# Two 64-row turns of a recurrent attention and FFN kernel on VectorE in 32x32 blocks

## Chip, cores and metric

The kernel runs on one core of a Trainium2 chip. The metric is the device time of one execution in microseconds: 785.76 us before the change, the median of three runs (785.73 to 786.29). A change under 0.2%, some 1.6 us, is about the least that such a measurement can tell.

## What is computed

An attention of the RWKV7 kind with a state of 40x40 per batch and head, over 768 steps, and then an FFN on its output, all in float32 (4 batches, 8 heads, D = 40, 3072 tokens of 320 features, 2048 hidden):

```python
for t in range(S):                                  # S = 768
    y[:, :, t] = einsum('bhd,bhde->bhe', rt, state)
    Sa = einsum('bhde,bhe->bhd', state, at)
    state = state * wt[:, :, None, :] - einsum('bhd,bhe->bhde', Sa, bt)
    state = state + einsum('bhd,bhe->bhde', vt, kt)
x = y.transpose(0, 2, 1, 3).reshape(B * S, H * D)   # 3072 x 320
h = x @ w_in                                        # 320 x 2048
g = h * clip(h + 3.0, 0.0, 6.0) / 6.0
out = g @ w_out                                     # 2048 x 320
```

## The kernel before

The steps are cut into chunks of 64. A **unit** is one chunk of two batches, with their 8 heads; there are 24 units (0 to 23), four to a group of 128 steps (two chunks by two batch pairs), six groups. Tokens lie on the 128 partitions (64 of each batch), so what is loaded has to be turned until the 40 features of a head lie on the partitions: two heads side by side, in slots of 64 rows. In the main loop (units 4 to 23 as `own`) such turns are TensorE transposes. `turn_pairs` (L486) does 128x128 at a time, four to a unit, for W, K and the state; `turn_halves` (L496) does 64x64 at a time in 64-row tiles, eight to a unit, for R, V, A and B.

A unit's work is in stages. **Ahead** of its turn: W (turn of w, two scans by VectorE that give the cumulative gammas), gam (gammas `gam` and inverse gammas `rgam`, by POOL), A (L609: turned a times gam, `at`), B (turned b times rgam), K, F and E (masked scores), factor (L664: the inverse gammas turned back, times k and b by POOL), EV. The 32x32 blocks of a whole group are inverted by VectorE (`invert`, with 60 dependent operations at L769 and L775 between transposes at L749, L778 and L783), spread over the work of other units, and joined by TensorE in 32-row tiles. **Own** stages, which need the state of the unit two before: RT (L857: turn of r, copied by ACT at L862, and the fading of the state, by POOL and VectorE), VT (turn of v), R, C, S, U, UT, rS, H, ysn (L1021: 64 matmuls that give the new state and the output), then `move` and `move2` (L1068, L1073): 4 and 4 DMAs that lay the unit's output out as the FFN's input `xt`.

**The FFN** is a stream of 48 jobs, half the hidden width of one unit each. `expand` (L1118 to L1153) is 16 matmuls of 128x128x128 and, for the last 64 of the 320 features, 8 "short" ones (`short`, L1128) in 64x128 tiles, two tiles in turn; then relu and a minimum with product by ACT (L1139) and VectorE (L1140) into `gt`. `contract` (L1165) is matmuls of 320 columns from `gt`. `feed` puts pieces of this stream between the blocks of attention work, at rates written by hand.

**The order** is written by hand (a manual schedule). The loop has four blocks to a unit (BLOCKS), and in each, `a_block` collects the stages that fall due by OWN_STAGES (from the unit's first block), AHEAD_STAGES or CLOSE_STAGES and hands them to `together`. That issues TensorE's products in the order of PRODUCTS: first those of TURNS (W, S, K) in 128-row tiles, then at FIRST_NARROW the short matmuls of the expand before, then the products in 64-row tiles. What follows the products (evacuations by VectorE, ACT and POOL, and DMA issues) is issued in the order of RESULTS, as soon as five PSUM banks would be passed or the block's products are out. Each engine works through its own queue in order.

**DMAs** of the loop are nearly all issued by SyncE (SP), one queue in order: `fetch` (L452 to L471) loads R and V in four DMAs (L467) and W, A, B and K in two (L470); each single-buffered tile is fetched for the next unit right after its last use in the code, so R in RT, A in A, B, K and V in factor. The xt moves and the output stand in the same queue. Before the loop, a plan by hand (PLAN) works through group 0 and prepares group 1; the fetch of R for unit 4 stands in it at BEGIN + 2.

Of the kernel before, what the change touches and what calls it, by code (L numbers as in the profile page):

```python
# [31 lines left out]
def kernel(  # L32
# [183 lines left out]
    inputs, others = {}, {}  # L216
    for name in "WABK":
        inputs[name] = padded(const.tile([P, H, SLOT], F32, name=name), name)
    seconds()
    for name in "BK":  # L220
        others[name] = second(name)
# [9 lines left out]
    inputs["R"] = padded(const.tile([P, H, SLOT], F32, name="R"), "R")  # L231

    RR = const.tile([P, 2, NPR * D + SLOT - D], F32, name="RR")
    nc.gpsimd.memset(RR[:, :, NPR * D:], 0.0)
# [209 lines left out]
    def fetch(name, i, engine=None):  # L444

        if i is None or i >= NK:
            return
        x, crossed = {"W": (w, 0), "A": (a, 0), "B": (b, 0), "K": (k, 0), "R": (r, 1),
                      "V": (v, 1)}[name]
        if name == "V":  # L450
            t = values[i % AHEAD]
        else:  # L452
            t = placed.get((name, i))
            if (name, i) == ("R", 1):
                t = others["K"]
            if (name, i) == ("W", NU + 1):
                t = values[NU]
            t = t if t is not None else (others if i < 2 * NU and i % 2 and name != "R" else inputs)[name]
        g, p = names[i]
        engines = engine or nc.sync  # L460
        for q in range(2):
            engine = engines[q] if isinstance(engines, tuple) else engines
            y = x[2 * p + q, :, g * BL:(g + 1) * BL, :]
            rows = slice(q * BL, (q + 1) * BL)
            if crossed:
                for s in range(2):
                    engine.dma_start(out=t[rows, 4 * s:4 * s + 4, 0:D],  # L467
                                     in_=y[s::2].rearrange("h t e -> t h e"))
            else:
                engine.dma_start(out=t[rows, :, 0:D], in_=y.rearrange("h t e -> t h e"))  # L470
        data[i][name + "N"] = t  # L471
# [29 lines left out]
    def by_banks(x):  # L501
        return x[:].rearrange("p r (q t) -> p q r t", q=2)

    def turn_in(x, halves):

        return turn_halves(x)[2:] if halves else [turn_pairs(x)]
# [25 lines left out]
    def begun_beside():  # L532

        begin = -(-(SCAN + 1) // 16) * 16
        for n, name in enumerate("KB"):
            x = area[:, begin + n * H * JOIN:begin + (n + 1) * H * JOIN]
            nc.gpsimd.memset(x, 0.0)
            beside[name] = x.rearrange("p (h t) -> p h t", h=H)
        beside["E"] = grp.tile([P, H, BL], F32, name="E", tag="U", bufs=1)
        nc.gpsimd.memset(beside["E"][:], 0.0)  # L540

    def masked(o, x=None):
        if x is None:
# [6 lines left out]
    def prepare(i, F):  # L550
# [25 lines left out]
        def gam_stage():  # L576

            prods, wm = o["prods"], o["wm"]
            first = start[:].rearrange("p (n i) -> p n i", i=HB + 1)[:, :, 0]
            nc.vector.reciprocal(first, prods[:].rearrange("p r m i -> p (r m) i")[:, ::-1, HB])  # L580
            back = _ap(wm, SCAN, [[-1, SCAN]])
            nc.vector.tensor_tensor_scan(out=back, data0=back, data1=start[:], initial=0.0,  # L582
                                         op0=ALU.mult, op1=ALU.add)
            nc.vector.memset(first, 1.0)
            gam = o["G"] = grp.tile([P, NPR, P], F32, name="gam", tag="gam", bufs=NU + 2)
            rgam = o["rg"] = placed.get(("rgam", i)) or tmp.tile([P, NPR, P], F32, name="rgam", bufs=2)
# [12 lines left out]
            nc.gpsimd.tensor_copy(gv[:, :, HB:BL], o["prods"][:, :, 1, 0:HB])  # L599
            nc.gpsimd.tensor_copy(rv[:, :, 0:HB], o["prods"][:, :, 0, 0:HB][:, :, ::-1])  # L600
            dec = grp.tile([P, 2, 2, NPR], F32, name="dec", tag="dec", bufs=NU + 2)
            nc.gpsimd.tensor_copy(dec[:].rearrange("p m q r -> p r q m"),
                                  o["prods"][:].rearrange("p (r q) m i -> p r q m i", q=2)[:, :, :, :, HB])
            o["dec"] = dec
            if NU + 1 < i <= 2 * NU:
                fetch("V", i)
            yield from ()

        def a_stage():  # L609
            x = turn_in(o["AN"], halves)  # L610
            yield PE
            nc.vector.memset(_ap(o["wm"], 0, [[HB + 1, 2 * NB + 1]]), 0.0)  # L612
            at = o["at"] = grp.tile([P, NPR, P], F32, name="at", tag="at")
            for y, z, g in zip(parts_of(at, halves), x, parts_of(o["G"], halves)):
                nc.vector.tensor_tensor(out=y, in0=z, in1=g, op=ALU.mult)
            fetch("A", following(i))

        def b_stage():
# [45 lines left out]
        def factor_stage():  # L664
# [23 lines left out]
            for x, name in enumerate("KB"):  # L688
# [5 lines left out]
            if i > 2 * NU:  # L694
                fetch("V", i)
            for name in "BK":
                fetch(name, following(i))

        def k_stage():
            x = turn_pairs(o["KN"])  # L700
            yield PE
            kt = o["kt"] = turned("kt")
            nc.vector.tensor_tensor(out=kt[:], in0=x[:], in1=o["rg"][:], op=ALU.mult)

        def e_stage():
            x = scores(o["kt"], o["at"])
# [141 lines left out]
    def step(i):  # L848
# [6 lines left out]
        m = {}  # L855

        def s_RT():  # L857
            x = turn_in(o["RN"], halves)
            yield PE
            m["RT"] = turned("RT")  # L860
            for y, z in zip(parts_of(m["RT"], halves), x):
                nc.scalar.activation(out=y, in_=z, func=AF.Copy)  # L862
            if i and i != NU - 1:
                fetch("R", i + 1)
            if fresh:
                nc.gpsimd.tensor_copy(last_dec[p][:], dec[:, 1])
                return
# [2 lines left out]
            nc.gpsimd.tensor_copy(last_dec[p][:], dec[:, 1])  # L870
            nc.vector.tensor_tensor(out=st[:, :, :, 0:D], in0=st[:, :, :, 0:D],
                                    in1=_ap(scale[:], 0, [[NPR, 2], [1, NPR], [0, D]]), op=ALU.mult)

        def s_R():

# [195 lines left out]
        def s_move2():  # L1071
            for dst, src in m["moves"][4:]:
# [1 line left out]
            ready[i] = m["xt"]  # L1074
            yield from ()

        return {"RT": s_RT, "R": s_R, "VT": s_VT, "S": s_S, "U": s_U, "C": s_C, "UT": s_UT,
                "rS": s_rS,
                "sn": s_sn, "ysn": s_ysn, "H": s_H, "y": s_y, "move": s_move, "move2": s_move2}

# [37 lines left out]
    def expand(xt, j0, gts):  # L1118
# [6 lines left out]
                             stop=(begun[c] == 3 * NQ - 1))  # L1125
            begun[c] += 1

        def short():  # L1128
            narrow.clear()
            for i in range(NQ):  # L1130
                for c in range(2):
                    add(c, i, win2[half(c), (j0 + i) * P:(j0 + i + 1) * P], xt[half(c), 2, :])
            if begun[0] + begun[1] == 6 * NQ:
                results()

        def results():
            for c in range(2):
                gt = ffn.tile([P, NQ, P], F32, name="gt", bufs=5)
                nc.scalar.activation(out=gt[:], in_=hp[c][:], func=AF.Relu, bias=three[:], scale=1.0)  # L1139
                nc.vector.scalar_tensor_tensor(out=gt[:], in0=gt[:], scalar=6.0, in1=hp[c][:],  # L1140
                                               op0=ALU.min, op1=ALU.mult)
# [252 lines left out]
    for _ in range(18):  # L1394
# [21 lines left out]
    FIRST_NARROW = PRODUCTS[len(TURNS)]  # L1416

    def together(stages):

# [35 lines left out]
    def a_block(m):  # L1455

        if coming and begins[coming[0]] == m:
            u = coming.popleft()
            close = coming and begins[coming[0]] < m + BLOCKS
            ahead[u, m] = prepared(u), CLOSE_STAGES if close else AHEAD_STAGES  # L1460
        if m % BLOCKS == 0 and m // BLOCKS + NU < NK:
            i = m // BLOCKS + NU
            own[i, m] = step(i), OWN_STAGES
        parts = {}, {}
        for (u, begin), (fs, order) in sorted(own.items()) + sorted(ahead.items()):
            if m - begin < len(order):
                for name in order[m - begin]:
                    parts[begin % BLOCKS > 0].setdefault(name, []).append(fs[name])
# [15 lines left out]

    m = 0
    begun_beside()
    for i in range(NU, NK):
        spread[0] = i >= 2 * NU - 1
        for j in range(BLOCKS):
# [58 lines left out]
```

## Time and profile before

| | |
|---|---|
| Median of three runs | 785.76 us |
| The profiled execution | 785.4 us |
| Its span (first to last instruction) | 783.7 us |
| Mean granted TensorE clock | 0.965 |
| VectorE stream transposes L749, L778, L783 (128x1024), mean | 2.16, 1.97, 2.05 us |
| L496 turns of R, of A (TensorE matmuls of 64x64) | 160, 128 |
| ACT copies of the turned R, L862 | 22 of 0.597 us |
| SP's issue of one fetch DMA, median, L467 / L470 | 0.608 / 0.633 us |
| Fetches of R / of A in the whole kernel | 92 / 37 DMAs |

How to read the views: the page gives each engine's busy time and share of the span, and then, in 40 slices of about 19.6 us, the busy share of each in tenths. PE is TensorE's matmuls, PEld its weight loads, which run beside them; PEclk is the clock that TensorE was granted, in tenths. Lines such as L1021 are those of the kernel printed above. A list of waits gives what an engine stood idle for, with the instruction that released it: us in total, times, longest. A timeline has the start in us, the length, engine, line and operation with its tiles, and "x8" for eight records drawn as one; a group's records overlap, so its length and the start of the next group can differ. SPq is SP's queue of DMA issues.

### The profile page before, as it was taken

Reading aid. Unit: us, or ns where it says so; the run is one execution under the profiler, and the core shown is the slowest. Engines: PE = TensorE matmul, PEld = TensorE weight load, DVE = VectorE, ACT = ScalarE, POOL = GpSimd, SP = SyncE. Lnnn points to the kernel's source line nnn. Section 1 sums busy time; section 2 is a strip of 40 time slices with the busy share of each in tenths; the row PEclk is TensorE's granted clock in tenths of the full one; section 3 lists DMA queues with packets and bytes.
Section 4 is the critical chain, followed back from the end, with each engine's and each line's share of the span. In section 5 each row is a group of like instructions: output and inputs, shape, how many; then the busy total and the mean of one; then the engine's idle time right before and its main releaser. Section 6 shows DMA issues by size and latency. Waiting matters only on the chain.

```text
span 783.7 us, 32780 instructions
## 1 busy us (share of the span) xinstructions
PE 725.0 (93%) x14552; PEld 613.3 (78%) x14552; DVE 486.6 (62%) x951; ACT 320.2 (41%) x664; POOL 171.9 (22%) x321
## 2 busy tenths in 40 slices
PE   5636788999999989999999999999999999999998
PEld 3625677878878778888788888888888888888886
DVE  7899967688546699345888336887436972223110
ACT  2386865324445334443334543334543234412211
POOL 6403111222232304121304212203212111110000
PEclk9855899999999999999999999999999999999999
DMA  9684554311333312223213223213221101110000
GB/s 123 116 202 123 113 168 69 68 27 35 58 59 63 67 33 48 50 49 66 41 38 58 46 51 64 44 30 60 49 55 39 26 5 30 30 29 10 12 20 18
DMA packets 174205, 44.87 MB, mean 57 GB/s; under 512 B 157424, under 2 KB 172784, under 8 KB 174064
## 3 DMA queue, kind: packets, MB, share of 16 engines
q1 hardware_dynamic: 169760, 42.03, 27.5%
q8 instruction: 115, 1.88, 1.0%
q10 hardware_dynamic: 4304, 0.74, 0.6%
q14 instruction: 26, 0.21, 0.1%
HBM read 34.08 MB, written 3.93 MB: 49 GB/s over the span
## 4 chain that ended last, share of the span: by engine, by line
PE 77%; DVE 10%; issue 6%; DMA 2%; ACT 2%; POOL 2%; SPq 1%; POOLq 0%; ACTq 0%; DVEq 0%
PE h L1124 27%; PE o L1165 25%; PE pair L1021 4%; PE pair L524 4%; PE pair L496 2%; PE one L486 2%; DVE prods L571 2%; PE pair L884 2%; PE pair L925 1%; PE pair L717 1%; DVE prod L769 1%; PE pair L964 1%; DVE x L775 1%; PE pair L980 1%; PE one L906 1%
## 5 line engine op out<-in xcount | busy, mean ns | idle before, releaser
L1124 PE MATMUL h<-xt,win 128*128 128x128 f32 (+1 forms) x2304 | 248.7, 281 | 4.5 <-DVE gt L1140 4.5
L1124 PEld LDWEIGHTS h<-xt,win 128*128 128x128 f32 (+1 forms) x2304 | 229.3, 191 | 22.6 <-issue 4.2
L1165 PE MATMUL o<-wout,gt 128*128 128x320 f32 x768 | 230.5, 443 | 0.0
L1165 PEld LDWEIGHTS o<-wout,gt 128*128 128x128 f32 x768 | 138.4, 190 | 50.9 <-issue 0.2
L1140 DVE SCALAR_TENSOR_TENSOR gt<-gt,h 128x512 f32<-128x512 f32 x96 | 62.0, 680 | 73.4 <-ACT gt L1139 73.4
L1139 ACT ACTIVATE gt<-h,three 128x512 f32<-128x512 f32 x96 | 62.9, 687 | 102.8 <-PE h L1124 102.3
L546 DVE COPY_PREDICATED area<-mask,pair 128x512 f32<-128x512 int32 x56 | 40.4, 724 | 62.2 <-PE pair L524 52.8
L769 DVE TENSOR_TENSOR prod<-x 128x30 f32<-128x30 f32 (+9 forms) x180 | 65.5, 364 | 8.9 <-POOL x L754 3.3
L775 DVE TENSOR_TENSOR x<-x,prod 128x30 f32<-128x30 f32 (+9 forms) x180 | 64.3, 357 | 5.5
L1029 POOL TENSOR_TENSOR yg<-ys,gam 128x512 f32<-128x512 f32 x20 | 25.4, 1272 | 126.1 <-DVE ys L1028 83.2
L690 POOL TENSOR_TENSOR KBt<-K,rgt 128x320 f32<-128x320 f32 x22 | 19.1, 870 | 151.4 <-ACT rgt L679 139.9
L571 DVE TENSOR_TENSOR_SCAN prods<-area,start 128x528 f32<-128x528 f32 x24 | 40.8, 1703 | 9.7 <-ACT area L567 9.6
L1028 DVE TENSOR_TENSOR ys<-pair,ys 128x512 f32<-128x512 f32 x20 | 13.8, 690 | 49.8 <-PE pair L1021 40.8
L862 ACT ACTIVATE RT<-pair 128x512 f32<-128x512 f32 x22 | 13.1, 597 | 54.5 <-PE pair L496 54.4
L722 ACT ACTIVATE EV<-pair 64x320 f32<-64x320 f32 x44 | 18.9, 430 | 36.9 <-PE pair L717 36.5
L1021 PE MATMUL pair<-area,KBt 64*64 64x104 f32 x1280 | 33.1, 252 | 0.0
L1183 ACT ACTIVATE ob<-o 128x320 f32<-128x320 f32 x22 | 9.6, 437 | 56.2 <-PE o L1165 37.8
L837 ACT ACTIVATE tinv<-pair 32x256 f32<-32x256 f32 x48 | 18.0, 375 | 34.7 <-PE pair L827 34.2
L582 DVE TENSOR_TENSOR_SCAN area<-area,start 128x528 f32<-128x528 f32 x24 | 31.1, 1297 | 0.8
L1021 PEld LDWEIGHTS pair<-area,KBt 64*64 64x64 f32 x1280 | 29.1, 133 | 1.4
L950 POOL COPY area<-V 128x320 f32<-128x320 f32 x20 | 9.1, 455 | 84.6 <-DVE area L612 52.9
L600 POOL COPY rgam<-prods 128x256 f32<-128x256 f32 x22 | 24.9, 1131 | 0.0
(286 smaller groups left out, 1049.9 us busy)
## 6 DMA issues: line engine op xcount, KB each, us to landing
V<-in_v_dram SPq DMA_DIRECT2D x96, 40.0 KB
out_dram<-ob SPq DMA_DIRECT2D x47, 80.0 KB
R<-in_r_dram SPq DMA_DIRECT2D x92, 40.0 KB
B<-in_b_dram SPq DMA_DIRECT2D x42, 80.0 KB
K<-in_k_dram SPq DMA_DIRECT2D x42, 80.0 KB
W<-in_w_dram SPq DMA_DIRECT2D x37, 80.0 KB
A<-in_a_dram SPq DMA_DIRECT2D x37, 80.0 KB
xt<-yg SPq DMA_DIRECT2D x72, 40.0 KB
```

The costliest lines, as they stand in the source:

```text
L524: nc.tensor.matmul(out=o[i][half(q), n ^ (2 * q * placed), :], lhsT=lhs[half(i, D), n ^ (2 * q * swap), half(q)], rhs=rhs[half(i, D), n, h ...
L546: nc.vector.copy_predicated(out=x[:].rearrange("p (i h) t -> p i h t", i=2), mask=mask8, data=o[2])
L571: nc.vector.tensor_tensor_scan(out=prods[:].rearrange("p r m i -> p (r m i)"), data0=wm[:, 0:SCAN], data1=start[:], initial=0.0, op0=ALU.m ...
L582: nc.vector.tensor_tensor_scan(out=back, data0=back, data1=start[:], initial=0.0, op0=ALU.mult, op1=ALU.add)
L769: nc.vector.tensor_tensor(out=pv, in0=_ap(x[:], (i + 1) * L + i, [[L, n], [0, i]]), in1=_ap(x[:], i * L, [[0, n], [1, i]]), op=ALU.mult,)
L775: nc.vector.tensor_tensor(out=rest, in0=rest, in1=pv, op=ALU.add)
L1021: nc.tensor.matmul(out=both[q][half(s), pr, :], lhsT=o[name][half(q), h * D:h * D + SLOT], rhs=beside[name][half(q), 4 * rs + 2 * (s ^ (q ...
L1029: nc.gpsimd.tensor_tensor(out=yg[:], in0=m["ys"][:].rearrange("p r q t -> p r (q t)"), in1=o["G"][:], op=ALU.mult)
L1124: nc.tensor.matmul(out=hp[c][:, i, :], lhsT=lhsT, rhs=rhs, start=(begun[c] == 0), stop=(begun[c] == 3 * NQ - 1))
L1139: nc.scalar.activation(out=gt[:], in_=hp[c][:], func=AF.Relu, bias=three[:], scale=1.0)
L1140: nc.vector.scalar_tensor_tensor(out=gt[:], in0=gt[:], scalar=6.0, in1=hp[c][:], op0=ALU.min, op1=ALU.mult)
L1165: nc.tensor.matmul(out=op[:], lhsT=gts[c][:, n, :], rhs=wout[:, c * HJ + r * NQ + n, :], start=((split or r == 0) and c == 0 and n == 0), ...
```

## The change

- **R and A in another layout.** The tiles R and A get 640 columns. R of unit 4 and later and A of unit 8 and later are loaded with two tokens (80 floats) to a row and a second copy, shifted by 32 features, on other partitions, so that every 32x32 block of a head's 40 features lies where VectorE can turn it. R takes 8 DMAs to a unit instead of 4, A takes 4 instead of 2, all by SP.
- **VectorE turns them** (`turn_blocks`): R in two transposes of 128x256 straight into one buffer RT, A in one of 128x512 into `at`, which is then multiplied by gam in SBUF instead of from PSUM. TensorE's eight turns of each and ACT's copies of RT go.
- **Stages.** The fading of the state is a stage of its own (`fade`). `fade`, and then RT with VT, stand two blocks earlier, in the last blocks of the unit before: V's half turn is then in the block of the factor stage, whose turn of the inverse gammas has the same 64-row tiles. EV moves from the eighth to the fifth block of AHEAD_STAGES, V's fetch from the factor stage to the K stage, and RT stands near the end of RESULTS.
- **Short pieces in 64x64.** In blocks with none of the products VT, B and factor (HALVES) the 8 short matmuls become 16 of 64x64 tiles, the tile shape of the products that follow them. 19 of the 41 such groups in the loop do so.
- rgam and RT get single buffers in place of pools of two, and gt four buffers in place of five.

```diff
+        if name == "R" and i >= NU or name == "A" and i >= 2 * NU:
+            y = x[2 * p:2 * p + 2, :, g * BL:(g + 1) * BL, :]
+            n = 2 if name == "R" else 1
+            y = y.rearrange("q (k s j) t e -> s j (q k) (t e)", s=2, j=n).rearrange(
+                "s j k (l e) -> s j l k e", e=2 * D)
+            for s in range(2):
+                for c in range(0, D, L):
+                    z = s * SLOT + c
+                    to = rooms[name][z:z + L].rearrange("l (j k e) -> l j k e", j=n, e=2 * D)
+                    for j in range(n):
+                        nc.sync.dma_start(out=to[:, j, :, 0:2 * D - c], in_=y[s, j, :, :, c:])
+            data[i][name + "N"] = t
+            return
...
+    def turn_blocks(to, name):
+        x = rooms[name].rearrange("p (j k y e) -> p j k y e", j=2, y=2, e=D)[:, :, :, :, 0:L]
+        if name == "A":
+            nc.vector.transpose(out=to[:].rearrange("p r (q t y) -> p q r y t", q=2, y=2), in_=x)
+            return
+        for j in range(2):
+            nc.vector.transpose(out=to[:, 2 * j:2 * j + 2].rearrange("p r (q t y) -> p q r y t", q=2, y=2),
+                                in_=x[:, j].rearrange("p (q r) y t -> p q r y t", q=2))
...
         def a_stage():
-            x = turn_in(o["AN"], halves)
+            x = None if halves else turn_pairs(o["AN"])
             yield PE
             nc.vector.memset(_ap(o["wm"], 0, [[HB + 1, 2 * NB + 1]]), 0.0)
             at = o["at"] = grp.tile([P, NPR, P], F32, name="at", tag="at")
-            for y, z, g in zip(parts_of(at, halves), x, parts_of(o["G"], halves)):
-                nc.vector.tensor_tensor(out=y, in0=z, in1=g, op=ALU.mult)
+            if halves:
+                x = at
+                turn_blocks(at, "A")
+            nc.vector.tensor_tensor(out=at[:], in0=x[:], in1=o["G"][:], op=ALU.mult)
             fetch("A", following(i))
...
         def s_RT():
-            x = turn_in(o["RN"], halves)
-            yield PE
+            x = None if halves else turn_pairs(o["RN"])
+            yield PE
+            if halves:
+                m["RT"] = beside["RT"]
+                turn_blocks(m["RT"], "R")
+                fetch("R", i + 1)
+                return
...
+        def short(fours=False):
             narrow.clear()
             for i in range(NQ):
                 for c in range(2):
-                    add(c, i, win2[half(c), (j0 + i) * P:(j0 + i + 1) * P], xt[half(c), 2, :])
+                    y = win2[half(c), (j0 + i) * P:(j0 + i + 1) * P]
+                    if not fours:
+                        add(c, i, y, xt[half(c), 2, :])
+                        continue
+                    for z in range(2):
+                        nc.tensor.matmul(out=hp[c][half(z), i, :], lhsT=y[:, half(z)], rhs=xt[half(c), 2, :],
+                                         start=(begun[c] == 0), stop=(begun[c] == 3 * NQ - 1))
+                    begun[c] += 1
...
-    OWN_STAGES = [["RT", "VT"], ["R", "C", "S"], ["U", "UT", "rS"], ["H"], ["ysn"],
-                  ["move", "move2"]]
-    AHEAD_STAGES = [["W", "gam"], ["A", "B"], ["F", "K"], ["E", "factor"], [], [], [],
-                    ["EV"]]
+    EARLY_STAGES = [["fade"], ["RT", "VT"]]
+    OWN_STAGES = EARLY_STAGES + [[], ["R", "C", "S"], ["U", "UT", "rS"], ["H"], ["ysn"],
+                                 ["move", "move2"]]
+    AHEAD_STAGES = [["W", "gam"], ["A", "B"], ["F", "K"], ["E", "factor"], ["EV"]]
...
-    PRODUCTS = ["W", "S", "K", "RT", "VT", "A", "B", "factor",
+    PRODUCTS = ["W", "S", "K", "VT", "B", "factor",
                 "ysn", "EV", "R", "C", "U", "UT", "rS", "H", "E", "F"]
-    RESULTS = ["RT", "ysn", "W", "VT", "EV", "R", "S", "C", "A", "B", "move", "move2",
-               "U", "UT", "rS", "F", "K", "H", "E", "factor", "gam"]
+    RESULTS = ["ysn", "W", "VT", "EV", "R", "S", "C", "A", "B", "move", "move2",
+               "U", "UT", "rS", "F", "K", "fade", "H", "E", "factor", "RT", "gam"]
...
-            if name == FIRST_NARROW and narrow and spread[0] and stages:
-                narrow[0]()
+            if name == HALVES[0] and narrow and spread[0] and stages:
+                narrow[0](not any(x in stages for x in HALVES))
```

More of the change, by code (lines that the diff above doesn't have):

```diff
@@ L215, with roomy @@
         nc.vector.memset(t, 0.0)
-    inputs, others = {}, {}
+    inputs, others, rooms = {}, {}, {}
+    def roomy(name):
+        rooms[name] = const.tile([P, 2 * H * D], F32, name=name)[:]
+        nc.gpsimd.memset(rooms[name][:, H * SLOT:], 0.0)
+        return rooms[name][:, 0:H * SLOT].rearrange("p (h e) -> p h e", h=H)
     for name in "WABK":
-        inputs[name] = padded(const.tile([P, H, SLOT], F32, name=name), name)
+        inputs[name] = padded(roomy(name) if name == "A" else const.tile([P, H, SLOT], F32, name=name), name)
     seconds()
@@ L230 @@
     values = [padded(const.tile([P, H, SLOT], F32, name=f"V{i}"), f"V{i}") for i in range(AHEAD)]
-    inputs["R"] = padded(const.tile([P, H, SLOT], F32, name="R"), "R")
+    inputs["R"] = padded(roomy("R"), "R")
     RR = const.tile([P, 2, NPR * D + SLOT - D], F32, name="RR")
@@ L540, in begun_beside @@
         nc.gpsimd.memset(beside["E"][:], 0.0)
+        for name in "rgam", "RT":
+            beside[name] = tmp.tile([P, NPR, P], F32, name=name, tag="rgam", bufs=2)
     def masked(o, x=None):
@@ L585, in gam_stage @@
             gam = o["G"] = grp.tile([P, NPR, P], F32, name="gam", tag="gam", bufs=NU + 2)
-            rgam = o["rg"] = placed.get(("rgam", i)) or tmp.tile([P, NPR, P], F32, name="rgam", bufs=2)
+            rgam = o["rg"] = beside["rgam"] if halves else placed.get(("rgam", i)) or \
+                tmp.tile([P, NPR, P], F32, name="rgam", bufs=2)
             gv = gam[:].rearrange("p r (q i) -> p (r q) i", q=2)
@@ L693, in factor_stage @@
                 )
-            if i > 2 * NU:
-                fetch("V", i)
             for name in "BK":
@@ L703, in k_stage @@
             nc.vector.tensor_tensor(out=kt[:], in0=x[:], in1=o["rg"][:], op=ALU.mult)
+            if i > 2 * NU:
+                fetch("V", i)
         def e_stage():
@@ L857, in s_RT, with s_fade @@
         def s_RT():
-            x = turn_in(o["RN"], halves)
+            x = None if halves else turn_pairs(o["RN"])
             yield PE
+            if halves:
[3 more added lines that the diff above has]
+                return
             m["RT"] = turned("RT")
-            for y, z in zip(parts_of(m["RT"], halves), x):
-                nc.scalar.activation(out=y, in_=z, func=AF.Copy)
+            nc.scalar.activation(out=m["RT"][:], in_=x[:], func=AF.Copy)
             if i and i != NU - 1:
                 fetch("R", i + 1)
+            yield from s_fade()
+        def s_fade():
             if fresh:
@@ L872, in s_RT @@
                                     in1=_ap(scale[:], 0, [[NPR, 2], [1, NPR], [0, D]]), op=ALU.mult)
+            yield from ()
         def s_R():
@@ L1075, in s_move2 @@
             yield from ()
-        return {"RT": s_RT, "R": s_R, "VT": s_VT, "S": s_S, "U": s_U, "C": s_C, "UT": s_UT,
+        return {"RT": s_RT, "fade": s_fade, "R": s_R, "VT": s_VT, "S": s_S, "U": s_U, "C": s_C, "UT": s_UT,
                 "rS": s_rS,
@@ L1126, in add @@
             begun[c] += 1
-        def short():
+        def short(fours=False):
             narrow.clear()
@@ L1137, in results @@
             for c in range(2):
-                gt = ffn.tile([P, NQ, P], F32, name="gt", bufs=5)
+                gt = ffn.tile([P, NQ, P], F32, name="gt", bufs=4)
                 nc.scalar.activation(out=gt[:], in_=hp[c][:], func=AF.Relu, bias=three[:], scale=1.0)
@@ L1415 @@
     BLOCKS = 4
-    FIRST_NARROW = PRODUCTS[len(TURNS)]
+    HALVES = PRODUCTS[len(TURNS):6]
     def together(stages):
@@ L1460, in a_block @@
             ahead[u, m] = prepared(u), CLOSE_STAGES if close else AHEAD_STAGES
-        if m % BLOCKS == 0 and m // BLOCKS + NU < NK:
-            i = m // BLOCKS + NU
+        i, early = (m + len(EARLY_STAGES)) // BLOCKS + NU, m + len(EARLY_STAGES)
+        if m >= 0 and early % BLOCKS == 0 and i < NK:
             own[i, m] = step(i), OWN_STAGES
@@ L1467, in a_block @@
                 for name in order[m - begin]:
-                    parts[begin % BLOCKS > 0].setdefault(name, []).append(fs[name])
+                    parts[(u, begin) in ahead and begin % BLOCKS > 0].setdefault(name, []).append(fs[name])
         for k, part in enumerate(parts):
@@ L1486 @@
     begun_beside()
+    own[NU, -len(EARLY_STAGES)] = step(NU), OWN_STAGES
+    for _ in in_turn(own[NU, -len(EARLY_STAGES)][0], [x for stages in EARLY_STAGES for x in stages]):
+        pass
     for i in range(NU, NK):
```

## The prediction

> **What bounds the kernel now.** I read the page's busy lines and slices first, then TensorE's waits from 185 us to the end, then the timeline of single turns and of one unit's way into the FFN. The page:
>
> ```profile
> PE 725.0 (93%) x14552; PEld 613.3 (78%) x14552; DVE 486.6 (62%) x951; ACT 320.2 (41%) x664; POOL 171.9 (22%) x321
> PE   5636788999999989999999999999999999999998
> DVE  7899967688546699345888336887436972223110
> PEclk9855899999999999999999999999999999999999
> ```
>
> After the ninth slice TensorE is at 9 in nearly every one, with the clock at 9 or more. VectorE reaches 8 or 9 only in the stretches with an inversion. TensorE's waits from 185 us on (us in total, times, longest):
>
> ```profile
> PE h L1124 <- DVE gt L1140: 1.9, 3, 0.8
> PE pair L717 <- issue: 1.5, 1, 1.5
> PE pair L980 <- ACT UT L970: 1.1, 1, 1.1
> PE pair L884 <- DVE E L546: 1.0, 1, 1.0
> PE pair L717 <- DVE area L612: 0.5, 1, 0.5
> PE pair L827 <- DVE area L612: 0.5, 2, 0.3
> ```
>
> These six lines are 6.5 us of 600. So TensorE's own stream sets the end: each microsecond taken out of it counts, and each new wait of TensorE counts too, since nothing later is idle to absorb it. The profiled execution took 785.4 (span 783.7 and 1.7 around it), 0.05% under the median of 785.76. A sum of differences holds for both; I apply it to the median.
>
> **1. TensorE loses turns: −8.8 us.** Timeline of TensorE, 559 to 563 us:
>
> ```profile
> 559.59 0.60 PE L486 MATMUL one<-ident,W 128*128 128x128 f32 x4
> 560.12 0.47 PE L496 MATMUL pair<-ident,R 64*128 64x64 f32 x8
> 560.42 0.42 PE L496 MATMUL pair<-ident,V 64*128 64x64 f32 x8
> 560.76 1.66 PE L1021 MATMUL pair<-area,KBt 64*64 64x104 f32 x64
> ```
>
> Records overlap, so a group's price is the distance of starts. V's eight turns go from 560.42 to 560.76 = 0.34, R's take 0.30, and both hold a small wait; groups that follow without one take 0.243 to 0.248. I use 0.245. R leaves TensorE in 20 units and A in 16: 36 × 0.245 = 8.8 (by 0.30 it would be 10.8). V's half turn stays and only changes place.
>
> **2. Tile changes: −2.0 us.** From a group's last record to the next group, where both use one shape, TensorE takes 57 ns here; where the shape changes, 148 to 202: about 0.095 more. Counted in the two built programs, the main loop changes shape 287 times before and 266 after, 21 × 0.095 = 2.0. [...]
>
> **3. Pieces in 64x64: 0.** In 19 blocks the eight 64x128 pieces of an expand (0.86 to 1.0 us) become sixteen 64x64 pieces of 128 columns. The nearest row is L1021 above: 64 matmuls of 64x64 tiles with 104 columns in 1.6 us, 25 ns each, four at a time. For 128 columns that is 31 ns, with two matmuls per old piece (32 in all): 0.95. So nothing, if four overlap. If only two did, +0.9 each.
> [...]
>
> **4. VectorE gains the turns: 0 by themselves.** Nearest rows: L778 turns 128x1024 in 1.97 us (source in order, output with a step, as here), L749 in 2.16. A's 512 elements: 1.03; R's two of 256: 1.1. 20 × 1.1 + 16 × 1.03 = 39 us more on VectorE, 62% to 67%, and ACT loses R's 20 copies of 0.6. VectorE's own idle time takes it, but for the inversion at 266 to 302 us, where the slices show 8 to 9 and I give back 0.5 of TensorE's gain. The gt waits at 390.6 and 506.1 (0.77 each) follow results of EV in the old place and lose 0.5 each. Net −0.5.
>
> **5. SP's queue gets A's fetch behind VectorE: +7.5 us.** The way of unit 15 into the FFN:
>
> ```profile
> 541.59 0.47 PE L496 MATMUL pair<-ident,A 64*128 64x64 f32 x8
> 542.08 1.96 SPq L470 DMA_DIRECT2D A<-in_a_dram  x2
> 543.88 0.72 DVE L546 COPY_PREDICATED area<-mask,pair 128x512 f32<-128x512 int32 x1
> 544.13 3.14 SPq L1068 DMA_DIRECT2D xt<-yg  x4
> 544.51 0.67 DVE L615 TENSOR_TENSOR at<-pair,gam 128x512 f32<-128x512 f32 x1
> 550.67 0.60 PE L1124 MATMUL h<-xt,win 128*128 128x128 f32 x3
> ```
>
> Before, the tile A is free when TensorE has turned it (542.0), and SP issues its two DMAs at 542.08, ahead of the unit's four xt moves. After, A is free only when VectorE has turned it. In RESULTS, that turn stands behind C's mask (ends at 544.60 here), and the A fetch is four DMAs. SP works in order, so the xt moves stand behind. First move = end of the mask + 0.05 + the turn 1.03 + 0.12 + four issues 4 × 0.65 (L470's median is 0.633, L467's 0.608) + 0.1 = +3.9 us. The moves land 4.26 after the first issue begins (544.13 to 548.4), so xt is there 8.16 after the mask's end. The first expand of the unit begins 6.07 after it (550.67 − 544.60). Units with an A fetch ahead in the same block, with that distance, corrected for what steps 1 and 4 take out of the stretch (−0.3 for A's turn on TensorE; +0.49 for 7, 11 and 15, whose chain to the mask starts earlier by R's and V's turns): 7: 6.41 → 6.6; 10: 7.31 → 7.0; 11: 6.14 → 6.33; 14: 7.30 → 7.0; 15: 6.07 → 6.26. TensorE waits 1.6 + 1.15 + 1.8 + 1.15 + 1.9 = 7.6, taken as 7.5. Units 8, 9, 12, 13 and 16 have 8 to 12 us and do not wait; from 17 on no A is fetched. If the moves land faster by 0.8 each the sum is 3.5; if VectorE runs 0.7 late in each it is 11.
>
> **6. Before the loop: +2.6 us.** SP issues without a pause from 117 to 151 us, and TensorE already waits for B at its end:
>
> ```profile
> 149.84 0.63 PE L486 MATMUL pair<-ident,B 128*128 128x128 f32 x4 [0.27 <-DMA B<-in_b_dram]
> ```
>
> R of unit 4 (four issues at 129.5) now takes eight, ahead of that B: 4 × 0.65 = 2.6 later. Nothing absorbs it after, as TensorE is full from there (bounds 1.0, if the queue's order there loosens, to 3.5).
>
> **7. What costs nothing.** R's fetches in the loop: 26 DMAs per unit become up to 32, 32 × 0.65 = 21 us in a unit of some 24.5, so SP keeps up, with 3 us to spare. Without that cover each DMA too many is 0.65 per unit. Two POOL memsets at the start (0.26 for R's existing one) lie beside the first loads. One gt buffer fewer: an expand's gt are used up before the next but one begins. V's fetch, moved from factor to k, issues earlier and has its half turn a block later. EV now waits for V's DMA and VectorE's turn of A; each is there a block before.
>
> **Sum:** −8.8 − 2.0 − 0 − 0.5 + 7.5 + 2.6 = −1.2 → 784.6. Own range 781 to 787.5, from step 5's 3.5 to 11 and step 6's 1.0 to 3.5, not both at an end.
>
> **Rivals.**
> - *The moves are in time.* If the moves land before the expands (VectorE reaches the turn earlier, or the FFN has slack that I read as none), steps 5 and 6 shrink to 0 to 2.6: 785.76 − 11.3 + 0 to 2.6 = 774.5 to 777. For: units 8, 9, 12 and 13 show 8 to 12 us. Against: unit 15's 6.07. Chance 0.25.
> - *SP falls behind (slower).* SP holds xt, R, V, B and K in one queue; R's fetch now waits for VectorE too. Where such a wait meets an inversion (266 to 302, 501 to 526), VectorE comes late by up to one pass of its queue, and the eight R DMAs (5.2 us) stand ahead of moves and V. It decides from 3 us lost per unit, SP's margin; with 1 us lost beyond it in 8 of 20 units (the inverting ones), +8 on top of the sum: 792 (789 to 795). For: SP full before the loop. Against: 3 us margin. Chance 0.18.
> - *VectorE's turn is cheap.* If it cost like an ordinary 128x512 operation (L615: 0.67), each of the five waits loses 0.35: 782.9. Chance 0.04. [...]
> - *Four tiles do not overlap (slower).* Step 3 then costs 19 × 0.86 = 16: 801. Against: L1021's 25 ns. Chance 0.05.
>
> **Chances.** Main case 0.48 (0.21 under 784.2, 0.18 within, 0.09 above 787.3), moves in time 0.25, SP behind 0.18, cheap turn 0.04, no overlap 0.05. A difference under 0.2%, 1.6 us, is about what a measurement of this kernel cannot tell from none. Faster 0.21 + 0.25 + 0.04 = 0.50, same 0.18, slower 0.09 + 0.18 + 0.05 = 0.32. The range holds the main case, most of the first rival and half of the second: 775.5 to 791.
>
> **What would show it.** Step 1: TensorE's R and A groups of 64x64 gone, busy time down by some 9 us. Step 3: expand's short groups still 0.9 to 1.0 us. Step 4: new transposes of 1.03 and 0.55. Step 5: TensorE waits for xt's DMA at L1124 in units 7, 10, 11, 14 and 15, 1 to 2 us each; none, and the time is near 775. Step 6: the wait for B at about 150 us grows from 0.27 to some 2.9. It is wrong if VectorE becomes what TensorE waits for in many places, or if the first expands move in the order.

## The result, and the profile after

The changed kernel takes 779.05 us, the median of four runs (778.37 to 779.86), against 785.75 before: a ratio of 0.9915 (95% interval 0.9898 to 0.9932). Its profiled execution took 778.37 with a span of 776.6, that is 7.1 less span than before. The page's busy line, and TensorE's waits from 170 us to the end (us in total, times, longest):

```profile
PE 714.2 (92%) x14568; PEld 604.4 (78%) x14568; DVE 508.0 (65%) x1007; ACT 310.1 (40%) x644; POOL 176.4 (23%) x323
```

```profile
PE h L1167 <- DMA xt<-yg: 4.2, 3, 1.8
PE pair L752 <- DVE area L645: 1.9, 1, 1.9
PE pair L862 <- DVE area L645: 1.5, 1, 1.5
PE h L1167 <- DVE gt L1190: 1.4, 3, 0.7
PE pair L1023 <- ACT UT L1013: 1.1, 1, 1.1
PE pair L554 <- DVE E L578: 0.6, 1, 0.6
```

TensorE is busy 10.8 us less. Its waits are 10.7 instead of 6.5, and the whole difference is the first line, the wait for xt that the prediction asked for. The other five lines sum to the same as before: one wait for ACT of 1.1 in both, and 5.4 in the rest (1.9 + 1.5 + 1.4 + 0.6 for VectorE, against 1.9 + 1.5 + 1.0 + 0.5 + 0.5, where the list puts the 1.5 at L717 down to no engine).

Times of one kernel scatter by some us from run to run: the changed kernel took 777.9 to 785.1 in a later series, the kernel before 785.0 to 791.0. So the three runs within 0.6 us from which 0.2% was taken as the least difference were closer than usual. In the traces most of that scatter lies before 170 us: the contraction that starts at 170.35 in the profile after starts between 169.4 and 176.6 in the traces below. So I also use a **stretch** that leaves this out: from that contraction to the last output copy.

```profile
170.35 4.57 PE L1215 MATMUL o<-wout,gt 128*128 128x320 f32 x16
...
772.38 0.44 ACT L1233 ACTIVATE ob<-o 128x320 f32<-128x320 f32 x1 [7.88 <-issue]
```

After: 772.38 − 170.35 = 602.0. Before, the same two instructions start at 171.02 and 779.91: 608.9. So 6.9 of the 7.1 us lie in the stretch. For a kernel that ran only once, the stretch is what this document compares.

Within the stretch, more than the waits changed. Behind its longest wait (1.9 us, at L752), TensorE was granted half its clock for 3.4 us (0.50 from 280.28 to 283.69); the profile before has no such step in its stretch. The same sixteen matmuls, to the start of the next group, before and after, and then the stretch from 280 to 284 us after: its length, the busy times of PE, PEld, DVE, ACT and POOL with their counts, the granted clock, the DMA share and GB/s:

```profile
281.89 1.16 PE L1124 MATMUL h<-xt,win 128*128 128x128 f32 x8
282.89 2.32 PE L1165 MATMUL o<-wout,gt 128*128 128x320 f32 x8
285.04 0.60 PE L486 MATMUL one<-ident,K 128*128 128x128 f32 x4
```

```profile
280.18 2.02 PE L1167 MATMUL h<-xt,win 128*128 128x128 f32 x8
282.00 3.16 PE L1215 MATMUL o<-wout,gt 128*128 128x320 f32 x8
284.99 0.60 PE L506 MATMUL one<-ident,K 128*128 128x128 f32 x4
```

```profile
280.00:284.00 4.00, 4.00 (x33) 3.28 (x25) 3.72 (x9) 2.24 (x4) 0.97 (x4) 0.57 0.37 80
```

They take 3.15 us before and 4.81 after, so this **half-clock step** cost 1.7 us. A list of waits doesn't show it, and it has to be counted when stretches are compared.

Unit 15's way into the FFN, in the timeline after (start, length):

```profile
539.65 0.74 DVE L578 COPY_PREDICATED area<-mask,pair 128x512 f32<-128x512 int32 x1
540.30 0.69 DVE L528 STREAM_TRANSPOSE at<-A 128x512 f32<-128x512 f32 x1
541.02 1.80 SPq L478 DMA_DIRECT2D A<-in_a_dram  x4
542.92 3.12 SPq L1111 DMA_DIRECT2D xt<-yg  x4
548.17 2.02 PE L1167 MATMUL h<-xt,win 128*128 128x128 f32 x16 [1.82 <-DMA xt<-yg]
```

The order is the one foretold: the mask, VectorE's turn, A's four issues, the moves, and TensorE waiting for xt. But the moves start 2.5 us after the mask's end (540.39 to 542.92), not 3.9. The turn takes 0.69 and the four issues 1.8. In the other units of step 5 it is 2.5 (unit 10), 2.7 (11), 2.9 (14) and 3.7 (7, where the four issues take 2.9).

### The profile page after: what moved, and what is told of

It reads as the page before. It is cut to its first block, busy times and chain, and to the rows that moved or that the text cites. A ratio compares the mean times of both kernels' runs of the same rounds, so it can differ in the third digit from the quotient of the medians.

```text
span 776.6 us, 33024 instructions
## 1 busy us (share of the span) xinstructions
PE 714.2 (92%) x14568; PEld 604.4 (78%) x14568; DVE 508.0 (65%) x1007; ACT 310.1 (40%) x644; POOL 176.4 (23%) x323
## 4 chain that ended last, share of the span: by engine, by line
PE 71%; DVE 13%; SPq 5%; issue 4%; ACT 3%; DMA 3%; POOL 0%; DVEq 0%; ACTq 0%; POOLq 0%
PE h L1167 24%; PE o L1215 22%; PE pair L554 4%; PE pair L1064 4%; DVE prod L804 2%; PE h L1180 2%; DVE x L810 2%; SPq L490 2%; PE one L506 2%; DVE prods L603 2%; PE pair L927 1%; PE pair L1007 1%; PE pair L516 1%; PE pair L968 1%; PE pair L1023 1%
## 5 line engine op out<-in xcount | busy, mean ns | idle before, releaser
L1167 PE MATMUL h<-xt,win 128*128 128x128 f32 (+1 forms) x2000 | 228.9, 282 | 8.4 <-DMA xt<-yg 4.2
L1167 PEld LDWEIGHTS h<-xt,win 128*128 128x128 f32 (+1 forms) x2000 | 211.9, 192 | 24.2 <-issue 7.7
L804 DVE TENSOR_TENSOR prod<-x 128x30 f32<-128x30 f32 (+9 forms) x180 | 63.8, 354 | 8.9 <-POOL x L789 2.5
L938 ACT ACTIVATE VT<-pair 128x512 f32<-128x512 f32 x22 | 13.1, 597 | 30.2 <-PE pair L705 16.2
L931 DVE TENSOR_TENSOR RR<-pair,EV 128x320 f32<-128x320 f32 x22 | 10.7, 486 | 20.8 <-PE pair L554 14.8
```

Of the source, the lines that this page charges most:

```text
L804: nc.vector.tensor_tensor(out=pv, in0=_ap(x[:], (i + 1) * L + i, [[L, n], [0, i]]), in1=_ap(x[:], i * L, [[0, n], [1, i]]), op=ALU.mult,)
L1167: nc.tensor.matmul(out=hp[c][:, i, :], lhsT=lhsT, rhs=rhs, start=(begun[c] == 0), stop=(begun[c] == 3 * NQ - 1))
```

## The experiments

### a_late: A's fetch behind the moves

```diff
 # a_stage
-            fetch("A", following(i))
+            if i < 2 * NU:
+                fetch("A", following(i))
 # k_stage, one block later
+            if i >= 2 * NU:
+                fetch("A", following(i))
```

> The changed kernel, with A's fetch for the main loop's units issued in the K stage, one block later, so that it stands behind the unit's xt moves in SP's queue. Theory (TensorE's waits for xt at L1167, 4.2 us in units 7, 11 and 15, come from A's four issues and VectorE's turn ahead of the moves): the three waits go, 779.05 - 4.2 = 774.9 us, 774.2 to 775.6. Rival (the moves land late by themselves, or the next wait takes their place at once): 777.5 to 779.5.

Measured: 776.32 us (six runs), 0.9866 of the kernel before (0.9837 to 0.9895); run again as a_late2, 774.39 and 0.9848 (0.9819 to 0.9876):

> a_late once more, beside r4_only: 0.9866 of the kernel before. If the two edits of best add up, the ratios of r4_only and a_late2 to the control's 0.9927 multiply to that of best (0.9818); if most of best's gain is R's, a_late2 comes out near 0.990.

The first time lies between the ranges of the theory and the rival, the second in the theory's; the traces decide. The stretch is 598.9 and 597.0, and neither trace holds a wait for xt. So those waits came from A's fetch ahead of the moves, which had no cause of their own to be late. Of the 1.9 us between the two traces, 1.4 are other waits, for VectorE and for one fetch of B. The 0.5 left is less than the 1.7 of a half-clock step, so by this estimate both traces have as many; a_late's lies at about 203 to 207 us, where the clock is 0.68.

### a_pe: A turned by TensorE again

```diff
-            x = None if halves else turn_pairs(o["AN"])
+            x = turn_in(o["AN"], halves)
...
-            if halves:
-                x = at
-                turn_blocks(at, "A")
-            nc.vector.tensor_tensor(out=at[:], in0=x[:], in1=o["G"][:], op=ALU.mult)
+            for y, z, g in zip(parts_of(at, halves), x, parts_of(o["G"], halves)):
+                nc.vector.tensor_tensor(out=y, in0=z, in1=g, op=ALU.mult)
...
-    PRODUCTS = ["W", "S", "K", "VT", "B", "factor",
+    PRODUCTS = ["W", "S", "K", "VT", "A", "B", "factor",
```

The edit also gives A its old layout in `fetch` and counts A's products among HALVES.

> The changed kernel, with A turned by TensorE again and fetched in the old layout in two DMAs; R stays with VectorE. Theory: TensorE gets 16 groups of turns back, 16 x 0.245 = +3.9, its count of tile changes stays at 266, and the waits for xt (4.2) go, since A's tile is free once TensorE has turned it: 779.05 + 3.9 - 4.2 = 778.8, so that A's half of the change is worth nothing as it stands. Rival (the waits for xt do not hang on A's fetch): 779.05 + 3.9 = 783.0.

Measured: 779.54, ratio 0.9906 (0.9881 to 0.9932), a stretch of 601.7, and no wait for xt. Right: A's half of the change earns nothing as it stands, since it makes the wait that eats it. TensorE's work at full clock grows by 4.2 us (the account below), 0.26 for each of the 16 groups.

### both_pe: both turned by TensorE, the stages where the change puts them

A as above, and in RT TensorE's turns and ACT's copies back in place of `turn_blocks`, with R in its old layout too.

> The changed kernel, with R and A turned by TensorE and fetched in the old layouts; the stages' new places and the short pieces in 64x64 stay. Theory: 36 x 0.245 = +8.8 and -4.2 for the waits for xt: 783.7 (782.9 to 784.5). Rival (the gain comes from the stages' new places and the shorts, and TensorE's turns of R and A lay in time that it waits anyway): 775 to 780.

Measured: 826.63, ratio 1.0497 (1.0462 to 1.0531). Neither theory. TensorE's waits in its trace:

```profile
PE pair L554 <- ACT rgt L712: 23.8, 12, 4.1
```

L554 is there the E stage's product, in the block that has R's and V's half turns, the factor's turn, H and E. By `together`'s rule, a block's products are cut off where they need more than five banks. R and V fill one pair of banks, the factor's turn and H a second, and E's pair would be the sixth bank, so TensorE waits for all that was begun. Without R, V shares its pair with the factor's turn, H shares with E, and four banks do. That is read in the code and fits the line; it was not tried alone. So the total time does not price the turns. If that reading holds, V's half turn can only move there because R has left TensorE. The stretch is 45.8 over the profile after, and only 20.4 of that is idle time of TensorE: 15.0 are lost in nine more half-clock steps, most of them behind such waits, and 10.4 are TensorE's work (the account below).

### no_turns: the kernel before without the 36 groups of turns

```diff
-            x = turn_in(o["RN"], halves)
+            x = [VN[:].rearrange("p (r q) t -> p q r t", q=2)] if halves else turn_in(o["RN"], halves)
...
-            x = turn_in(o["AN"], halves)
+            x = [o["BN"][:].rearrange("p (r q) t -> p q r t", q=2)] if halves else turn_in(o["AN"], halves)
```

> The kernel before, without TensorE's turns of R (20 units) and A (16 units): ACT's copy and VectorE's product read the unturned v and b instead, so the output is not the reference's; the fetches, copies and the order of stages stay. It prices the turns alone. By the prediction's 0.245 each the stretch (608.9 before) goes to 600.1. Rival (the groups that follow take over part of the cost of entering the tile shape, as the accounts of the profile after and of a_pe suggest, 7.0 for all 36): 601.9. If the turns lay in time that TensorE waits anyway: 608 to 609.

Measured: a stretch of 604.2, 4.7 less. TensorE's waits from 170 us on are 8.7 instead of 6.5:

```profile
PE pair L717 <- issue: 2.5, 1, 2.5
PE pair L827 <- DVE bt L623: 2.2, 4, 1.4
PE pair L650 <- issue: 1.7, 1, 1.7
...
PE pair L1021 <- DVE bt L623: 0.3, 1, 0.3
```

Behind the wait of 2.5 us this trace, too, has a half-clock step: the sixteen matmuls that took 3.15 us before take 4.82 here. So the turns' own work was 4.7 + 2.2 + 1.7 = 8.6 us (8.7 with the short gaps, in the account below), 0.24 for each of 36 groups, as the prediction priced it. Without these added waits and the clock's loss the stretch would be 600.3, where the prediction's price gives 600.1. The rival does not hold: the product of state and `at` (L884 before, L927 after), which follows the turns of A and B, takes 9.75 us in 20 groups before and 9.85 after from start to start, without the waits of the groups behind it. The kernel ran once, so this rests on one trace.

### no_fours: all short pieces in 64x128

```diff
-                narrow[0](not any(x in stages for x in HALVES))
+                narrow[0]()
```

> The changed kernel, with all short groups in 64x128 tiles. TensorE changes its tile shape 285 times in the loop instead of 266. Theory (a change costs 0.095 and the sixteen 64x64 pieces cost what the eight cost): 19 x 0.095 = +1.8, 780.9. Rival (twice the matmuls cost more than the change saves): 776 to 779.

Measured: 788.01 (twelve runs), ratio 0.9998 (0.9973 to 1.0022); the stretch is 606.9, 4.8 over the profile after. The direction was right and the size was not. One block of no_fours, and the same block after:

```profile
584.75 0.60 PE L506 MATMUL one<-ident,W 128*128 128x128 f32 x4
585.28 1.16 PE L1167 MATMUL h<-xt,win 64*128 64x128 f32 x16
586.37 1.66 PE L1064 MATMUL pair<-area,KBt 64*64 64x104 f32 x64
587.85 0.62 PE L752 MATMUL pair<-V,E 64*64 64x40 f32 x32
```

```profile
580.80 0.60 PE L506 MATMUL one<-ident,W 128*128 128x128 f32 x4
581.33 1.10 PE L1180 MATMUL h<-xt,win 64*64 64x128 f32 x32
582.25 1.61 PE L1064 MATMUL pair<-area,KBt 64*64 64x104 f32 x64
583.68 0.62 PE L752 MATMUL pair<-V,E 64*64 64x40 f32 x32
```

From start to start, the short group takes 1.09 in 64x128 and 0.92 in 64x64, and the group behind it 1.48 and 1.43. The 19 groups in 64x64 all take 0.92 to 0.93. That is 0.22 for each of 19, 4.1 us; the waits for xt differ by 0.7 more (4.9 against 4.2), and both traces have one half-clock step. By the ratios to the kernel before, no_fours is 5.6 to 6.5 us slower than the changed kernel, somewhat more than the stretch's 4.8; why is open. So the shorts in fours were about as large a part of the gain as A's and R's turns are after A's waits are paid (8.7 less 4.2).

### micro: what a transpose and an issue cost

Behind the end of the changed kernel, on idle engines: transposes of 128x512 with the output's elements n apart, and fetches in both layouts.

```diff
+    for _ in range(2):
+        turn_blocks(beside["RT"], "A")
+        ...
+        for n in 2, 4, 8, 16:
+            nc.vector.transpose(out=flat.rearrange("p (a t y) -> p a y t", t=L, y=n),
+                                in_=line.rearrange("p (a y) t -> p a y t", y=n))
+    ...
+    fetch("R", NK - 1)
+    fetch("A", NK - 1)
```

> The changed kernel with measuring work behind its end: transposes of 128x512 on the idle VectorE with the output's elements 1, 2, 4, 8 and 16 apart (two of each), and four fetches of r and two of a in the old layouts, eight of R and four of A in the new ones, on an idle SP. The total time is that much longer and means nothing. Theory (a transpose's price hangs on how far apart it writes): 0.69 at a distance of 2, less or the same at 1, and about 1.0 at 16, as L778's 1.97 for 1024 has it. Rival (price by size alone, with a fixed part that the large ones do not show): 0.69 at every distance. For the issues: theory (the layout sets the price) 0.60 to 0.65 in the old and 0.43 to 0.50 in the new one; rival (the state of the queue set it) the same for all.

Measured: 0.71 at distances 1 and 2, 1.08 to 1.10 at 4, 1.10 to 1.11 at 8, 1.04 to 1.05 at 16. The three lines of the transposes (least, median, most ns) are the change's form, a dense output, and n of 2 to 16; and SP's queue:

```profile
L528 DVE STREAM_TRANSPOSE RT<-A x2: 703/707/711, 770.5 to 776.9; 128x512 f32<-128x512 f32 x2
L1576 DVE STREAM_TRANSPOSE RT<-A x2: 711/711/711, 771.3 to 777.6; 128x512 f32<-128x512 f32 x2
L1579 DVE STREAM_TRANSPOSE RT<-R x8: 712/1062/1108, 772.8 to 782.1; 128x512 f32<-128x512 f32 x8
```

```profile
778.74 2.73 SPq L1586 DMA_DIRECT2D K<-in_r_dram  x4
781.51 1.58 SPq L1590 DMA_DIRECT2D B<-in_a_dram  x2
783.19 3.89 SPq L478 DMA_DIRECT2D R<-in_r_dram  x8
787.12 1.91 SPq L478 DMA_DIRECT2D A<-in_a_dram  x4
```

For these 128x512 transposes the price hangs on how far apart the output is written, with a jump between 2 (0.71) and 4 (1.08 to 1.10). In the loop the change's own turns cost 0.69 (A, 512 elements) and 0.42 (R, 256): 0.27 for 256 more elements, so by estimate 1.05 ns each and 0.15 fixed. The rows L778 (1.97 for 1024 elements) and L749 (2.16), from which the 1.03 was taken, write 32 elements apart. The issues are the layout's too: four of r in the old one take 2.73 on an idle queue, eight in the new one 3.89, 0.68 against 0.49 each with the gaps.

### r4_only, best and control

```diff
 # r4_only: before the loop
-            fetch("R", NU)
...
     for _ in second_group:
         pass
+    fetch("R", NU)
```

`best` is this edit and that of a_late together; `control` is the changed kernel once more.

> The changed kernel itself once more, unchanged, to have it on the same chip and in the same rounds as the next: all theories expect 0.9915 of the kernel before, within its interval, and from the first contraction at about 170 us to the last output copy 602.0 us as in the profile after (608.9 before).

> The changed kernel with only the fetch of R for unit 4 moved behind the preparation of group 1; A's fetch stays ahead of the xt moves. Theory (R's eight issues, 3.9 us, hold back B and K, and so TensorE at about 150 us, by 0 to 1.9 us from run to run): the wait for B is gone, the waits for xt stay, 0.5 to 2 us under the control (0.990 to 0.992 of the kernel before, control 0.9927). If it also takes away the slower clock that follows TensorE's wait at about 198 us in some runs (0.66 in the control's trace): up to 1.6 more. Rival (nothing there costs anything): 0.9927.

> The changed kernel with A's fetch in the K stage (as in a_late) and the fetch of R for unit 4 moved behind the preparation of group 1, so that no R stands ahead of B and K in SP's queue before the loop. Theory: the three waits for xt go (stretch from the contraction at about 170 us to the last copy 598.9, as in a_late), and before it the waits for B at about 150 us go, 0.3 to 1.9 us as they differ from run to run: 3 to 5 us under the control. Rival (R's eight issues never cost anything there): 3 us under the control, no less before the loop.

| | us, median | ratio to before (95%) | stretch | wait for B, about 150 us | waits for xt |
|---|---|---|---|---|---|
| control | 780.57 | 0.9927 (0.9900 to 0.9954) | 602.6 | 1.1 | 2.4 |
| r4_only | 780.11 | 0.9898 (0.9873 to 0.9924) | 603.0 | none | 2.9 |
| a_late, a_late2 | 776.32, 774.39 | 0.9866, 0.9848 | 598.9, 597.0 | 0.4, 1.5 | none |
| best | 772.53 | 0.9818 (0.9799 to 0.9837) | 596.0 | none | none |

`best` is 1.8% under the kernel before and beats the changed kernel. That is 8.0 under the control, more than the 3 to 5 foretold; the control's stretch has two half-clock steps (3.4 us), that of best none. The edit of R takes the wait for B away in both traces that have it, while the other traces of kernels with the change show 0.4 to 1.9, but for the profile after, which shows none. R's eight issues are not the whole cause: both_pe, with R's four old ones, waits 0.8 there. In both traces with the edit a half-clock step follows the wait for the mask at about 163 us (the four matmuls and the product behind it take 1.72 and 1.09 us in best and 2.50 and 1.09 in r4_only, 1.34 and 0.68 in the control), so from the turn of the inverse gammas at some 135 us to the contraction they need 36.8 and 36.4 us, the control 36.8. The edit's worth by time (0.9898 against 0.9927) is within the intervals' overlap, so of its own size no more can be said than 0 to some 4 us. That both edits add up fits: 0.9927 × (0.9898 / 0.9927) × (0.9848 / 0.9927) = 0.982.

## Why the prediction was right, and where not

The time, 779.05, lies in the stated range of 775.5 to 791, and faster was the likeliest sign. But that range spans the rivals as well. The sum for the main case, 784.6, was 5.6 too high, and its own range of 781 to 787.5 was missed, toward the rival in which the moves are in time.

This is where the time of the stretch went. TensorE's idle time is the stretch less its busy time; the loss to the half clock is an estimate, half of its busy time in the half-clock steps (half of 3.41 in the one at 280 us after, where the sixteen matmuls took 1.66 longer); what is left is its work at full clock:

| | stretch | idle | lost to half clock | work at full clock |
|---|---|---|---|---|
| before | 608.9 | 6.8 | 0 | 602.1 |
| after | 602.0 | 11.3 | 1.7 | 589.0 |
| control | 602.6 | 9.7 | 3.4 | 589.4 |
| best | 596.0 | 7.6 | 0 | 588.4 |
| a_pe | 601.7 | 8.5 | 0 | 593.2 |
| no_turns | 604.2 | 9.1 | 1.7 | 593.4 |
| no_fours | 606.9 | 12.0 | 1.7 | 593.2 |
| both_pe | 647.8 | 31.7 | 16.7 | 599.4 |

After, the control and best turn the same groups on the same engines, and their work agrees within 1.0 us, though their stretches differ by 6.6. By the steps, for the profiled execution:

| Step | foretold | measured | by |
|---|---|---|---|
| 1, turns leave TensorE | −8.8 | −8.7 | no_turns, 602.1 to 593.4 |
| 2 and 3, tile changes and shorts in 64x64 | −2.0 | −4.1 | no_fours |
| 4, waits for VectorE | −0.5 | 0 | 5.4 us before and after |
| 5, waits for xt | +7.5 | +4.2 | a_late |
| 6, before the loop | +2.6 | none in this profile | wait for B 0 here, up to 1.9 in other traces |
| not foretold: half clock at 280 us | 0 | +1.7 | 4.81 against 3.15 us |

−8.7 − 4.1 + 0 + 4.2 + 1.7 = −6.9, the stretch's difference. **Step 1** was right in mechanism and size, 0.24 for a group against 0.245. **Steps 2 and 3** were too small: they took a change of shape as 0.095 and the shorts as equal. In fact a short group in 64x64 is 0.17 faster where the blocks' next products have that shape, and the next group 0.05. The fourth rival (four tiles that do not overlap) is refuted: 0.92, not 1.8. **Step 4** charged 0.5 for VectorE, and the waits for it did not grow. But the one at about 280 us, 1.5 before and 1.9 after, was followed by a half-clock step in the profile after. The prediction has no term for the clock, and the step does not follow the same wait in every trace: it does in the profile after and the control, not in best and a_late (last section).

**Step 5** is the term that failed most, by size: "the turn 1.03" was 0.69 and "four issues 4 × 0.65" was 1.8 in most units, so that the moves mostly start 2.5 to 2.9 after the mask and not 3.9. The mechanism was right, and so were the distances to the first expand. With the landing 4.4 after the first issue, units 10 and 14, foretold at 1.15 each, just escape: in unit 10 xt is there some 6.95 after the mask and the expand comes after 7.1. Units 7, 11 and 15 wait 1.66, 0.72 and 1.82 (foretold 1.6, 1.8 and 1.9). That two of the three come out as foretold is chance. In unit 7 the issues were slow (the moves start 3.7 after the mask; 2.5 in the control, which does not wait there), and in unit 15 xt lands 5.25 after the first issue; why is open for both.

**Step 6** foretold a wait that this profile does not have. R's eight issues take 3.9, not 5.2, so that B was issued 1.3 later (144.04 against 142.72), not 2.6, and TensorE came to that turn of B 0.9 later than before (150.74 against 149.84) without a wait. Other traces of the changed kernel and its variants that keep R's fetch there wait 0.4 to 1.9. The step's words "nothing absorbs it after" stand as far as the traces show: TensorE's wait for VectorE's mask at about 163 us is 1.4 to 1.6 in all but the profile after (1.3, in two parts), whether the wait for B before it is 0 or 1.9.

**The rivals.** SP did not fall behind: in the profile after, no wait of the loop names a fetch of R, V, K or B. The cheap turn, given 0.04, was the truth about the turn (0.69 against 0.67 supposed); it names part of the error of step 5, and the cheaper issues are the other part. The moves were not in time in the changed kernel; a_late is what that rival looks like, at 774 to 776, as the rival had it (774.5 to 777).

## What to carry to other kernels

When a step moves from one engine to another, price what stands behind it in the queue of whoever refills its buffer: here a saving of TensorE's 16 turns (4.2 us) was eaten by a DMA queue in which a refill, now free later, stood ahead of a transfer with a deadline, and moving that refill one block later gave it back (4.2 us of waits for xt went). Take a price from a row of the same access pattern, not of the same operation: the 128x512 transposes here took 0.71 us written 2 elements apart and 1.04 to 1.11 written 4 to 16 apart. And before a difference of two stretches is called the price of an edit, take out of both what was lost to waits and to the granted clock: without the clock's 1.7 us the turns here looked a fifth cheaper than they are.

## What the hardware showed that I had not expected

A wait of TensorE can cost more than itself, and not each time. The half-clock step at 280 us is one case: 1.7 us behind a wait of 1.9. Another: in the profile after and in the control's, TensorE waits 1.51 us at L862, at about 198 us. What follows takes 2.05 for 16 matmuls after, and 2.98 in the control. The two traces from 198 to 202 us (columns as above), after and control:

```profile
198.00:202.00 4.00, 3.32 (x90) 3.11 (x92) 3.04 (x7) 1.50 (x4) 0.51 (x2) 1.00 0.37 64
```

```profile
198.00:202.00 4.00, 4.00 (x75) 3.79 (x60) 1.97 (x4) 1.50 (x4) 0.23 (x2) 0.66 0.36 59
```

The clock was 1.00 in the one and 0.66 in the other, after the same wait, and the control loses 1.6 us there. a_late shows it too (0.68); best, which waits 1.2 there, and a_late2, which waits 1.5, do not (1.00). The wait of 1.9 us at about 280 us (L752) is the same in the profile after, the control, best and a_late: the sixteen matmuls behind it take 4.81 and 4.82 us in the first two, 3.15 in the other two. In both_pe the clock is 0.57 to 0.58 in the 4 us after waits of 1.4 to 4.1 us at about 305, 558 and 616 us, and 1.00 after one of 1.39 at 336. In the profiles before and after, each clock record lasts 3.41 us or a multiple of it, but for the last of each trace. In steps of 3.41 us, the two traces hold 412 full-clock steps with another behind them: all 8 in which TensorE idles for 55% or more are followed by one at half the clock, none of the 390 with under 30% is, and of the 14 between, 5 are. The step at 280 us is of the first kind: TensorE is busy for 1.50 of the 3.41 us before it. And a wait of 1.5 us, 44% of a step, was enough in the control and a_late. The scatter would agree with a wait that falls differently over these steps from run to run; that is an estimate from the counts, and no run tried it.
